# Branch prefetch hints for the experts' tile sizes, and the branch of the smallest tile put first where an expert ends

## The chip, the cores and the metric

The kernel runs on one core of a Trainium2 chip. The time is device microseconds of one execution, the median of several. Five engines take part, each with its own instruction stream: TensorE (PE in the profile, PEld for its weight loads and its sequencer), VectorE (DVE), ScalarE (ACT), GpSimd (POOL) and SyncE (SP).

## The reference

Causal block attention feeds a dense two-layer MLP, and its rows go through a top-1 mixture of eight experts. All is float32.

```python
def reference(...):
    x = attention(q, k, v)                       # 4 x 8 heads, 576 x 64 -> 2304 rows of 512
    h = x @ w_in; x = (max(h, 0) + alpha * min(h, 0)) @ w_out     # 512 -> 2048 -> 512
    logits = x @ w_gate                          # 8 experts
    expert = argmax(logits); gate = softmax(logits)[expert]
    for e in range(8):
        mask = expert == e
        if not mask.any():
            continue
        out[mask] = gate[mask] * (max(x[mask] @ w1[e], 0) @ w2[e])   # 512 -> 1024 -> 512
```

How many rows an expert gets depends on the data. With these inputs the experts get, from the largest to the smallest, 1366, 515, 296, 103 and 24 rows; three get none.

## The kernel before

Attention and the MLP are planned by a scheduler of the kernel's own (`Plan`) and are one straight run of instructions. The mixture behind it is written out by hand in `Experts.run`, with branches, and every branch is taken by all five engines, each for itself, on row counts that it has loaded into registers.

The experts are taken in order of their counts, r = 0 for the largest. An expert's rows are worked off in tiles: as many of 256 rows (`big`, `tile256`) as needed, and at its end one of 128 (`tile128`) or of 64 rows (`tile64`), which `small` picks. Three kinds of branches decide:

- `more` (L1157): has expert r more than 128 rows? If so a 256-row tile follows, otherwise `small`.
- `rest` (L1105): behind a 256-row tile, are there more than 128 rows left? If so another one, otherwise `small`.
- `few` (L1087): in `small`, are more than 64 rows left? If so the 128-row tile, otherwise the 64-row tile.

Besides, L1145 asks whether expert r has any rows, L1154 whether to load the weights of expert r + 2, L1093 (inside `small`) whether any row is left, and L1080 whether there is a next expert, whose rows are then fetched within the tile. Where a condition holds the code goes straight on; where it doesn't, the engine jumps over the whole arm. An arm that ends jumps over the other arm; that jump is in the profile as one more COMPARE_BRANCH of the arm's line.

The code is long because each (expert, tile, size) has its own copy. On TensorE a 256-row tile is some 310 instructions, one of 128 rows 115, one of 64 rows about 170; the 128- and 64-row copies for all places at which an expert may end stand behind the expert's chain of 256-row tiles.

With these counts the tiles are: five of 256 and one of 128 (r = 0), two of 256 and one of 64 (r = 1), one of 256 and one of 64 (r = 2), one of 128 (r = 3), one of 64 (r = 4). The first of them, tile (0, 0), is a straight piece ahead of the first branch.

Of the kernel before, what the change touches and what calls it, by code (L numbers as in the profile page):

```python
# [14 lines left out]
PSUM = bass.MemoryType.PSUM  # L15
DRAM = bass.MemoryType.DRAM
IOA = bass.IndirectOffsetOnAxis

P = 128
B, H, S, D = 4, 8, 576, 64  # L20
# [4 lines left out]
E, F2 = 8, 1024  # L25
# [646 lines left out]
class Route:  # L672
# [73 lines left out]
    def scatter(A, i):  # L746
        A.nc.gpsimd.indirect_dma_start(out=A.ml.info, out_offset=IOA(ap=A.si[:, i:i + 1], axis=0), in_=A.ig[:, i, :], in_offset=None)

# [74 lines left out]
class Experts:  # L823
# [58 lines left out]
    def fetch(A, r, j, base, rows=NT + 1):  # L882
        it = A.itile(r, j)
        A.nc.sync.dma_start(it, A.info[ds(base + 2 * P * j, 2 * P), :].rearrange("(h p) c -> p h c", p=P))
        for h in range(2):
            A.nc.gpsimd.indirect_dma_start(out=A.xg[:, h], out_offset=None, in_=A.x2[0:rows, :], in_offset=IOA(ap=it[:, h, 0:1], axis=0))

# [37 lines left out]
    def scatter(A, yo, it, h=0):  # L925
        n = yo.shape[0]
        A.nc.gpsimd.indirect_dma_start(out=A.out, out_offset=IOA(ap=it[0:n, h, 0:1], axis=0), in_=yo, in_offset=None, bounds_check=NT - 1, oob_is_err=False)  # L927

# [120 lines left out]
    def run(A, base, last, order, order_all):  # L1049

        nc = A.nc

        def reg(row, r, top):
            return nc.sync.value_load(order.ri[0:1, row, r:r + 1], min_val=0, max_val=top)

        def xpreps(r, j):
            return [lambda: A.xprep(r, j, 0), lambda: A.xprep(r, j, 1)]


        def nexts(r, j, b, nb):
            fs = xpreps(r, j) if b is not None else []
            if nb is not None:
                fs += [lambda: A.fetch(r + 1, 0, nb)] + [lambda: None] * (4 - len(fs)) + xpreps(r + 1, 0)
            return fs

        def big(r, j, b, jobs=(), nb=None):
            more = A.TOP[r] > 2 * P * (j + 1)
            if more:  # L1070
                A.fetch(r, j + 1, b)
            A.body(r, j, 2 * P, jobs, nexts(r, j + 1, b if more else None, nb))

        def small(r, j, n, jobs=(), nb=None, sure=False):

            def go(size):
                if nb is None:
                    A.body(r, j, size)
                    return
                with A.tc.If(ns[r + 1] > 0) as c:  # L1080
                    A.fetch(r + 1, 0, nb)
                    A.body(r, j, size, jobs, xpreps(r + 1, 0))
                with c.Else():
                    A.body(r, j, size)

            if A.TOP[r] - 2 * P * j > 64:
                with A.tc.If(n > 2 * P * j + 64) as c:  # L1087
                    go(P)
                with c.Else():
                    if sure:  # L1090
                        go(64)
                    else:
                        with A.tc.If(n > 2 * P * j):  # L1093
                            go(64)
            else:
                with A.tc.If(n > 2 * P * j):
                    go(64)

        def rest(r, j, n, b):
            if A.TOP[r] <= 2 * P * j:  # L1100
                return
            if A.TOP[r] <= 2 * P * j + P:
                small(r, j, n)
                return
            with A.tc.If(n > 2 * P * j + P) as c:  # L1105
                big(r, j, b)
                rest(r, j + 1, n, b)
            with c.Else():
                small(r, j, n)

        hold = {}

        def known():
            hold["e1"], hold["nb"] = reg(0, 1, E - 1), reg(2, 1, (E - 1) * NT)
            A.load_raws(1, hold["e1"])
            A.wtiles(1)

        def counts():
            _, hold["n"] = nc.values_load_multi_w_load_instructions(order.ri[0:1, 1, :], min_val=0, max_val=NT)

        A.body(0, 0, 2 * P, last + [lambda: A.fetch(0, 1, base), order_all, known, counts], [lambda: None] * 5 + xpreps(0, 1))
        nb = hold["nb"]
        e2, ns = reg(0, 2, E - 1), hold["n"]
        n0 = ns[0]

        def convs(r):
            return [lambda i=i: A.conv(r, i) for i in range(16)]

        def end():
            A.load_raws(2, e2)  # L1130

        with A.tc.If(n0 > 5 * P) as c:
            big(0, 1, base)
            big(0, 2, base, convs(1), nb)
            end()
            rest(0, 3, n0, base)
        with c.Else():
            with A.tc.If(n0 > 3 * P) as c:
                big(0, 1, base, convs(1), nb)
                end()  # L1140
                small(0, 2, n0)
            with c.Else():
                small(0, 1, n0, convs(1), nb, True)
                end()
        with ExitStack() as st:  # L1145
            for r in range(1, E):
                n, base = ns[r], nb
                st.enter_context(A.tc.If(n > 0))
                nb = reg(2, r + 1, (E - 1) * NT) if r < E - 1 else None
                jobs = convs(r + 1) if r < E - 1 else ()  # L1150

                def end():
                    if r < E - 2:
                        with A.tc.If(ns[r + 2] > 0):  # L1154
                            A.load_raws(r + 2, reg(0, r + 2, E - 1))

                with A.tc.If(n > P) as c:  # L1157
                    big(r, 0, base, jobs, nb)
                    end()
                    rest(r, 1, n, base)  # L1160
                with c.Else():
                    small(r, 0, n, jobs, nb, True)
                    end()


def moe_kernel(tc, q, k, v, w_in, w_out, alpha, w_gate, w1, w2, out):
    nc = tc.nc
    with ExitStack() as ctx:
# [112 lines left out]
        def fetch_rows():  # L1281
            ex = hold["ex"]
            it = ex.itile(0, 0)
            for h in range(2):
                nc.gpsimd.indirect_dma_start(out=ex.xg[:, h], out_offset=None, in_=x2[0:NT - G, :], in_offset=IOA(ap=it[:, h, 0:1], axis=0))

# [45 lines left out]
```

## Time and profile before

| | us |
|---|---|
| median of 3 runs | 1041.59 (1037.69 to 1044.52) |
| the profiled execution | 1040.76 |
| its span, first to last instruction | 1039.0 |
| TensorE busy | 934.6 (90%) |

The span is on one core, and the mean granted clock of TensorE is 0.938 of full. The rows of experts with branches begin some 755 us after the start of the span.

### The profile page before, as it was taken

To read this page: it belongs to the slowest core of one execution; us is meant where nothing else is said; L and a number is where in the kernel's file an instruction comes from. 1 tells how busy PE (TensorE), PEld (TensorE's weight loads), DVE (VectorE), ACT (ScalarE), POOL (GpSimd) and SP (SyncE) were. 2 spreads that over 40 slices of the span, in tenths; PEclk is the share of its full clock that TensorE was granted. 3 is DMA by queue.
4 is the path that set the end of the run, shared out by engine and by line. 5 is a ranking of instruction groups with operands and counts; after the bars stand their busy time and mean duration, and the time that the engine had idled before them with its cause. 6 is when DMAs were issued, how large, how long until landed. Compare 5 with 4: busy or idle time off the path is not lost. (4 is left out here: it accounts for less than half of the span.)

```text
span 1039.0 us, 18700 instructions
## 1 busy us (share of the span) xinstructions
PE 934.6 (90%) x6725; PEld 809.6 (78%) x6725; DVE 524.6 (50%) x1286; ACT 417.0 (40%) x1131; POOL 360.8 (35%) x429
## 2 busy tenths in 40 slices
PE   7884979999999999999999999998799999988554
PEld 6653868788788878888899999987688888877543
DVE  4898989554655645645443434455224314415130
ACT  5785554444544545545422121224124224325231
POOL 3556866332332333343322222232114212315030
PEclk8795998999899999999999999999999999999776
DMA  6553721112310121300010010033245212506110
GB/s 185 165 196 123 223 87 34 34 47 67 82 47 19 54 67 47 87 19 13 14 41 25 18 41 1 22 83 121 80 154 172 94 44 86 178 27 205 30 36 6
DMA packets 85296, 79.78 MB, mean 77 GB/s; under 512 B 53759, under 2 KB 65679, under 8 KB 85136
## 3 DMA queue, kind: packets, MB, share of 16 engines
q1 hardware_dynamic: 73984, 57.37, 19.0%
q0 software_dynamic: 4240, 11.56, 3.4%
q10 hardware_dynamic: 6912, 8.92, 2.4%
q8 instruction: 77, 1.26, 0.5%
q14 instruction: 83, 0.68, 0.2%
HBM read 63.49 MB, written 14.72 MB: 75 GB/s over the span
## 5 line engine op out<-in xcount | busy, mean ns | idle before, releaser
L578 PE MATMUL l<-xh,wi 128*128 128x256 f32 x1152 | 236.3, 290 | 1.9 <-DVE t L583 1.8
L578 PEld LDWEIGHTS l<-xh,wi 128*128 128x128 f32 x1152 | 191.6, 195 | 7.9 <-DVE t L583 2.7
L609 PE MATMUL acc<-wo,gh 128*128 128x512 f32 x576 | 191.7, 414 | 0.0
L578 PE MATMUL l<-xl,wi 128*128 128x256 f32 x576 | 165.3, 287 | 0.7 <-DVE xl L557 0.7
L589 POOL TENSOR_TENSOR gl<-t,gh 128x256 fp32r<-128x256 f32 x119 | 91.6, 770 | 193.9 <-ACT gh L586 163.0
L477 POOL TENSOR_SCALAR P<-P,sm 128x256 f32<-128x256 f32 (+4 forms) x89 | 102.2, 1152 | 162.4 <-DVE sm L450 70.2
L582 DVE TENSOR_SCALAR t<-l,al 128x256 f32<-128x256 f32 x144 | 69.5, 482 | 158.2 <-PE l L578 146.0
L586 ACT CAST gh<-t 128x256 fp32r<-128x256 f32 x144 | 58.5, 407 | 173.2 <-DVE t L583 75.5
L609 PE MATMUL acc<-wo,gl 128*128 128x512 f32 x288 | 113.9, 396 | 4.9 <-POOL gl L589 4.9
L578 PEld LDWEIGHTS l<-xl,wi 128*128 128x128 f32 x576 | 112.2, 195 | 4.6 <-DVE xl L557 1.3
L609 PEld LDWEIGHTS acc<-wo,gh 128*128 128x128 f32 x576 | 95.7, 190 | 16.1 <-issue 5.2
L465 PE MATMUL PT<-ident,P 128*128 128x128 f32 (+1 forms) x400 | 72.8, 297 | 27.3 <-DVE qlo L360 12.8
L470 ACT COPY F<-PT 128x256 f32<-128x256 f32 (+3 forms) x154 | 61.2, 415 | 74.3 <-PE PT L465 72.5
L465 PEld LDWEIGHTS PT<-ident,P 128*128 128x128 f32 (+1 forms) x400 | 48.7, 148 | 44.6 <-POOL P L477 10.9
L428 DVE TENSOR_REDUCE nb<-S 128x1 f32<-128x256 f32 (+4 forms) x160 | 70.9, 476 | 23.3 <-PE S L415 21.3
L499 PE MATMUL o<-F,v 128*64 128x128 f32 (+2 forms) x960 | 70.4, 279 | 2.3 <-ACT F L470 2.0
L609 PEld LDWEIGHTS acc<-wo,gl 128*128 128x128 f32 x288 | 54.3, 189 | 19.2 <-POOL gl L589 7.0
L442 ACT ACTIVATE P<-S,nb 128x128 f32<-128x128 f32 (+3 forms) x128 | 67.0, 532 | 5.6 <-DVE nb L428 3.0
L927 POOL DMA_INDIRECT out_dram<-yo,it x21 | 22.7, 1082 | 133.8 <-ACT yo L953 68.4
L499 PEld LDWEIGHTS o<-F,v 128*64 128x64 f32 (+1 forms) x960 | 50.0, 145 | 19.2 <-ACT F L470 5.5
L583 DVE SCALAR_TENSOR_TENSOR t<-l,t 128x256 f32<-128x256 f32 x144 | 61.1, 425 | 5.0
L880 DVE TENSOR_TENSOR e<-raw,e 128x512 fp32r<-128x512 f32 x44 | 39.8, 928 | 33.0 <-ACT e L879 33.0
(351 smaller groups left out, 1758.3 us busy)
## 6 DMA issues: line engine op xcount, KB each, us to landing
raw<-in_moe_w_dram SPq DMA_DIRECT2D x80, 256.0 KB
rawi<-in_moe_w_in_dram SPq DMA_DIRECT2D x16, 512.0 KB
rawo<-in_moe_w_out_dram SPq DMA_DIRECT2D x16, 512.0 KB
xr<-xT SPq DMA_DIRECT2D x9, 512.0 KB
v<-in_v_dram SPq DMA_DIRECT2D x32, 128.0 KB
x<-y ACTq DMA_DIRECT2D x16, 256.0 KB
xT<-xo ACTq DMA_DIRECT2D x16, 160.0 KB
q<-in_q_dram SPq DMA_DIRECT2D x20, 128.0 KB
```

What stands on the lines that cost most here:

```text
L428: nc.vector.tensor_reduce(pl["nb", p, c][:, j:j + 1], pl[Ss[j]][:, 0:N[j]], axis=AX.X, op=ALU.max, negate=True)
L442: nc.scalar.activation(pl[x][:, 0:N[j]], pl[Ss[j]][:, 0:N[j]], AF.Exp, bias=nb, scale=1.0, accum_out=pl["sm", p, c][:, j:j + 1])
L465: nc.tensor.transpose(pl[t][0:w, k], pl[x][:, P * k:P * k + w], A.K.ident)
L470: f(pl[F][:, 0:n], pl[t][:, 0:n])
L477: (nc.gpsimd if on == "POOL" else nc.vector).tensor_scalar(y, y, pl["sm", p, c][:, jj:jj + 1], None, op0=ALU.mult)
L499: nc.tensor.matmul(pl[o][r, 0:N], lhsT=v[0:w, 2 * kc + h], rhs=f, start=kc == 0, stop=kc == c, skip_group_check=True)
L578: nc.tensor.matmul(pl[l][:, 0:G], lhsT=a[:, c], rhs=b, start=k == 0 and j == 0, stop=k == 3 and j == 2)
L582: nc.vector.tensor_scalar(pl[t], x, 0.0, A.K.al[:, f:f + 1], op0=ALU.min, op1=ALU.mult)
L583: nc.vector.scalar_tensor_tensor(pl[t], x, 0.0, pl[t], op0=ALU.max, op1=ALU.add)
L586: nc.scalar.copy(pl[gh], pl[t])
L589: (nc.gpsimd if on == "POOL" else nc.vector).tensor_sub(pl[gl], pl[t], pl[gh].bitcast(F32))
L609: nc.tensor.matmul(pl[acc], lhsT=x[:, c], rhs=w, start=f == 0 and j == 0, stop=f == 15 and j == 2)
```

## The change

Each engine gets an instruction that announces a branch ahead of it (a branch prefetch hint), and for each one register operation that computes the condition from the row count. A hint is set for `few` and `more` of the next expert and for `few` and `rest` behind the tile, at the start of each 256-row tile, and for `few` and `more` of the next expert at the start of each 128- or 64-row tile. The conditions are those of the branches themselves, so that a hint says which way its branch will go. Besides, `few` asks the opposite question: the 64-row tile now follows its branch directly, and the 128-row tile stands behind it.

```diff
+        def hint(label, cond):
+            A.tc.mark_branch_hint_location(label, hint=cond, engines=ENGINES)
+
+        def hints(r, j):
+            if A.TOP[r] - 2 * P * j > 64 and (r, j) not in ((0, 0), (0, 1)):
+                hint(f"few{r}_{j}", hold["n"][r] <= 2 * P * j + 64)
+            if A.TOP[r] > 2 * P * j + P and j > (2 if r == 0 else 0):
+                hint(f"rest{r}_{j}", hold["n"][r] > 2 * P * j + P)
+            if j == 0:
+                hint(f"more{r}", hold["n"][r] > P)
...
         def big(r, j, b, jobs=(), nb=None):
             more = A.TOP[r] > 2 * P * (j + 1)
+            if r + 1 < E:
+                hints(r + 1, 0)
+            if more and (r, j) != (0, 1):
+                hints(r, j + 1)
...
             def go(size):
+                if r + 1 < E:
+                    hints(r + 1, 0)
...
             if A.TOP[r] - 2 * P * j > 64:
-                with A.tc.If(n > 2 * P * j + 64) as c:
-                    go(P)
-                with c.Else():
+                with A.tc.If(n <= 2 * P * j + 64, label=f"few{r}_{j}") as c:
                     if sure:
                         go(64)
                     else:
                         with A.tc.If(n > 2 * P * j):
                             go(64)
+                with c.Else():
+                    go(P)
...
-            with A.tc.If(n > 2 * P * j + P) as c:
+            with A.tc.If(n > 2 * P * j + P, label=f"rest{r}_{j}") as c:
...
-                with A.tc.If(n > P) as c:
+                with A.tc.If(n > P, label=f"more{r}") as c:
```

The change shifts line numbers by up to 20: in the changed kernel `few` is L1107, L1093 is L1111, L1080 is L1100, `more` is L1177, and the register operations of the hints are L1064.

First place: TensorE, the start of expert r = 2 (`more` and tile (2, 0)). In a tile's name the first number is j, the second the size.

```order
L1154 UNCONDITIONAL_BRANCH x2
L1145 COMPARE_AND_BRANCH
L1157 COMPARE_AND_BRANCH
L923 MATMUL l_0_256+_0_16350<-cxh_7054,e_0_8919 128x256
L923 MATMUL l_0_256+_0_16350<-cxl_7055,e_0_8919 128x256
```

The same place in the changed kernel:

```order
L1174 UNCONDITIONAL_BRANCH x2
L1165 COMPARE_AND_BRANCH
L1177 COMPARE_AND_BRANCH
L1064 REGISTER_ALU
L1347 BRANCH_PREFETCH_HINT
L1064 REGISTER_ALU
L1347 BRANCH_PREFETCH_HINT
L1064 REGISTER_ALU
L1347 BRANCH_PREFETCH_HINT
L924 MATMUL l_0_256+_0_18250<-cxh_7054,e_0_8919 128x256
```

Three pairs stand where `big` calls for four hints: those of `few` for a tile j above 0 have no instruction in the built program; the last pair of the three is `rest`'s.

Second place: TensorE, the end of the 128-row copy of tile (2, 1) and the start of its 64-row copy, before:

```order
L923 MATMUL Y_1_128_17530<-e_15_9193,hh_7060 128x512 x2
L923 MATMUL Y_1_128_17530<-e_15_9193,hl_7061 128x512
L1087 UNCONDITIONAL_BRANCH
L1093 COMPARE_AND_BRANCH
L1006 MATMUL H_1_64_0_17568<-e_0_8919,cxh_7056 128x256 x2
L1006 MATMUL H_1_64_0_17568<-e_1_8951,cxh_7056 128x256 x2
```

And the start of `small` for tile (2, 1) in the changed kernel:

```order
L1107 COMPARE_AND_BRANCH
L1111 COMPARE_AND_BRANCH
L1064 REGISTER_ALU
L1347 BRANCH_PREFETCH_HINT
L1064 REGISTER_ALU
L1347 BRANCH_PREFETCH_HINT
L1007 MATMUL H_1_64_0_19697<-e_0_8919,cxh_7056 128x256 x2
```

The 64-row tile has moved from behind the 128-row tile to right behind the branch.

Third place: TensorE, `small` for tile (3, 0), the 128-row tile of the fourth expert, before:

```order
L1087 COMPARE_AND_BRANCH
L1080 COMPARE_AND_BRANCH
L923 MATMUL H_0_128+_0_19122<-e_0_9445,cxh_7054 128x512 x2
L923 MATMUL H_0_128+_0_19122<-e_0_9445,cxl_7055 128x512
L923 MATMUL H_0_128+_0_19122<-e_1_9446,cxh_7054 128x512 x2
```

And after the change:

```order
L1107 COMPARE_AND_BRANCH
L1064 REGISTER_ALU
L1347 BRANCH_PREFETCH_HINT
L1064 REGISTER_ALU
L1347 BRANCH_PREFETCH_HINT
L1100 COMPARE_AND_BRANCH
L1007 MATMUL H_0_64+_0_21717<-e_0_9445,cxh_7054 128x256 x2
```

What followed the branch here was the 128-row tile that these counts run; now it is the 64-row tile, and the 128-row tile is reached by a jump over both 64-row copies.

## Rows read from the trace of the kernel before

**Rows 1.** The page, part 1: busy time and share of TensorE.

```profile
PE 934.6 (90%) x6725; PEld 809.6 (78%) x6725; DVE 524.6 (50%) x1286; ACT 417.0 (40%) x1131; POOL 360.8 (35%) x429
```

**Rows 2.** Waits, 845 to 1039 us: waiter, releaser, us in total, times, longest.

```profile
PE H L1006 <- issue: 21.7, 3, 11.6
...
PE H_128+_0_19122 L923 <- issue: 8.0, 2, 7.1
...
PE l_256+_0_16350 L923 <- ACT e L879: 1.7, 1, 1.7
...
PE l_256+_0_13102 L923 <- ACT yo L993: 1.0, 1, 1.0
```

**Rows 3.** Timeline of TensorE, four stretches: start, us, tile, [idle before <-releaser].

```profile
919.67 1.54 PE L1006 MATMUL H<-e,cxh 128*128 128x256 f32 x11 [2.73 <-issue]
...
965.23 0.98 PE L1006 MATMUL H<-e,cxh 128*128 128x256 f32 x3 [7.39 <-issue]
...
983.63 1.19 PE L923 MATMUL H_128+_0_19122<-e,cxh 128*128 128x512 f32 x2 [7.09 <-issue]
...
986.17 1.01 PE L923 MATMUL H_128+_0_19122<-e,cxh 128*128 128x512 f32 x2 [0.92 <-issue]
...
1011.63 1.62 PE L1006 MATMUL H<-e,cxh 128*128 128x256 f32 x6 [11.59 <-issue]
```

**Rows 4.** Single branches of TensorE's sequencer, by line: min/median/max ns, start.

```profile
L1105 PEldq COMPARE_BRANCH  x1: 3509/3509/3509, 912.6 to 912.6; - x1
L1087 PEldq COMPARE_BRANCH  x1: 3206/3206/3206, 916.2 to 916.2; - x1
L1105 PEldq COMPARE_BRANCH  x1: 4238/4238/4238, 956.2 to 956.2; - x1
L1087 PEldq COMPARE_BRANCH  x1: 4410/4410/4410, 960.5 to 960.5; - x1
L1093 PEldq COMPARE_BRANCH  x1: 3693/3693/3693, 974.4 to 974.4; - x1
L1157 PEldq COMPARE_BRANCH  x1: 4742/4742/4742, 978.3 to 978.3; - x1
L1087 PEldq COMPARE_BRANCH  x1: 65/65/65, 983.1 to 983.1; - x1
L1080 PEldq COMPARE_BRANCH  x1: 3568/3568/3568, 996.4 to 996.4; - x1
L1157 PEldq COMPARE_BRANCH  x1: 4388/4388/4388, 1000.5 to 1000.5; - x1
L1087 PEldq COMPARE_BRANCH  x1: 3328/3328/3328, 1004.9 to 1004.9; - x1
L1080 PEldq COMPARE_BRANCH  x1: 2962/2962/2962, 1008.3 to 1008.3; - x1
L1154 PEldq COMPARE_BRANCH  x6: 65/189/255, 891.4 to 1021.4; - x6
```

**Rows 5.** Instruction transfers on queue q8, 600 to 700 us and 975 to 1012 us: packets, MB, share.

```profile
q8 instruction: 5, 0.08, 0.3%
...
q8 instruction: 10, 0.16, 2.3%
```

**Rows 6.** Register operations of SyncE at one line: min/median/max ns.

```profile
L869 SPq FUSED_REGOPS  x16: 37/46/51, 937.5 to 959.3; - x16
```

**Rows 7.** Timeline of ScalarE, 977 to 1014 us.

```profile
1000.14 0.69 ACT L993 ACTIVATE yo<-Y_128+_19175,it 128x512 f32<-128x512 f32 x1
1013.80 0.37 ACT L1032 COPY s<-H 128x256 f32<-128x256 f32 x1 [12.97 <-PE H L1006]
```

**Rows 8.** Windows: stretch, us, busy of PE, PEld, DVE, ACT, POOL, then granted clock, DMA.

```profile
854.00:868.00 14.00, 13.22 (x61) 10.31 (x59) 1.38 (x2) 3.75 (x6) 1.01 (x1) 1.00 0.06 23
...
965.00:977.00 12.00, 11.32 (x80) 11.14 (x80) 1.64 (x5) 3.17 (x10) 0.00 (x0) 0.83 0.01 3
1011.00:1024.00 13.00, 11.91 (x80) 11.73 (x80) 1.64 (x5) 3.17 (x10) 0.00 (x0) 0.78 0.01 4
```

More of the change, by code (lines that the diff above doesn't have):

```diff
@@ L17 @@
 IOA = bass.IndirectOffsetOnAxis
+ENGINES = [getattr(mybir.EngineType, e) for e in ("PE", "DVE", "Activation", "Pool", "SP")]
 P = 128
```

## The prediction

> **What bounds the kernel now.** I read the page first: TensorE is busy for 90% of the span [rows 1], so only its idle time can be won, and the change touches only the last 120 us, where the experts of few rows lie. So the second view is the list of waits there [rows 2]. Two groups stand out, 21.7 us in three waits ahead of a 64-row tile's first product and 8.0 us in two waits ahead of the 128-row tile. Both carry the releaser "issue": no other engine and no transfer holds TensorE up, it has no instruction yet. The third view, TensorE's timeline, gives them places [rows 3]: I call them C (tile (1, 2), 2.73 us), E (tile (2, 1), 7.39), F (tile (3, 0), 7.09 and 0.92) and G (tile (4, 0), 11.59). Two smaller waits, B and D, stand at the start of a 256-row tile and end with ScalarE [rows 2].
>
> The fourth view says what the engine does meanwhile: single branches [rows 4]. One that doesn't jump takes 65 ns, a short jump up to 255 ns, and each jump over a tile's copy takes 2.96 to 4.74 us. Instruction transfers go with them: 5 packets of 16 KB in 100 us of straight code, 10 in 37 us of the branches around F and G [rows 5]. A far jump thus costs a fetch.
>
> The sequencer stands ahead of the matrix unit, and that hides a part. At C the first of two long branches starts at 912.6 while the unit has work until 919.67 − 2.73 = 916.94, a lead of 4.3 us; in the same way the lead is 1.6 us at E, 2.1 at F and 3.6 at G [rows 3, 4]. The long branches less this lead give the idle time: at E 4.24 + 4.41 − 1.6 = 7.0 of 7.39; at F 3.69 + 4.74 − 2.1 = 6.3, and with the step to the next code 7.09; at G 3.57 + 4.39 + 3.33 + 2.96 − 3.6 = 10.7 of 11.59.
>
> The Trainium skill ("Advanced Engine Details and Errata", Control Flow Timing) gives a compare-and-branch about 108 ns. The 65 ns rows agree with it in size, the 3 to 4.7 us rows don't; by it nothing here could be won and the time would stay at 1041.
>
> **The change, part by part.** Two edits act in different ways.
>
> *The order of the arms.* At C, E and G `few` finds at most 64 rows; it jumped, for 3.21, 4.41 and 3.33 us, and now falls through for 0.065 as it did at F [rows 4]. At F it is the other way round: 65 ns become a jump over two 64-row copies, 3.2 us by the nearest row (the jump at C), bounds 2.96 and 4.74. The 128-row tile (3, 0) is now last in its part, so that the jump at its end, L1080 at 996.4, crosses one copy of 115 instructions; I take it for short, 0.2 us in place of 3.57, and hold it possible that it stays. The second L1080, 2.96 at 1008.3, has in the changed code no arm of another size between it and its target, only the tile's other copy of 170 instructions; I take 0.2 here too, bounds 0.2 and 2.96.
>
> *The hints.* A hint can only save the fetch of a branch that jumps. These are `rest` at C and E (3.51, 4.24), `more` at F and G (4.74, 4.39) and the new jump of `few` at F. No row shows a hint at work. The bounds for a hinted jump are 0.2 us (code on hand, the short jump) and the full row. `rest`'s hint is the last one set in its tile, and a whole 256-row tile lies between it and its branch: I take 0.2. `more`'s hint is set one tile ahead and has another jump, L1111 or L1100, between itself and its branch; I assume that the code a hint has brought does not wholly survive that, and take the middle: 3.0 at F, 2.0 at G. `few` at F is announced ahead of `more` in the same tile; I assume that the later hint takes its place, and give it the full 3.2. These two assumptions are the choice that the sum rests on.
>
> *What the hints cost.* Three pairs at the start of a 256-row tile, two at the start of a small one. The nearest rows are a register operation, 46 ns [rows 6], and the branch of 65 ns [rows 4]. But from that branch's start at 983.1 to the first product at 983.63 are 0.5 us, so an instruction may cost more than its record. I take 0.12 each, 0.7 for three pairs and 0.5 for two, bounds zero (inside the lead) and 1.5. Within a tile a lead of 1.6 us or more hides it; where TensorE already waits for its instructions it does not: at F, B and D. Hints on the other four engines stand behind the same branches and have more slack there. No hint waits for anything, and no DMA issue changes its place.
>
> Now the places, each against its idle time:
> - C: the two branches fall from 6.7 us to 0.3, the lead of 4.3 covers them: −2.7.
> - E: from 8.65 to 0.3 and 0.5 of hints, the lead of 1.6 covers that, bar some 0.4: −7.0. The weights of tile (2, 1) are there since tile (2, 0), so nothing else is late.
> - F: −1.7 for `more`, +3.1 for `few`, +0.3 for the hints, −0.9 for the second wait, whose code is no longer the next in line: +0.8.
> - G: the chain falls from 14.2 to 2.5, below the lead. Next to be late is ScalarE: its last activation of tile (3, 0) ends at 1000.83, and then it has branches of its own before it can read the first H [rows 7]. If `more` takes it 2 to 2.5 us, TensorE loses 1 to 1.5 waiting for room: −10.1.
> - B and D: +0.7 each.
>
> Sum −17.6 us of idle time.
>
> *The clock.* Behind these idle stretches TensorE's granted clock is lower: a 64-row tile with its 80 products is busy for 11.32 us at 0.83 behind E and 11.91 at 0.78 behind G, while a tile without an idle stretch ahead of it ran at 1.00 [rows 8]. Busy time times clock is 9.4 and 9.3, so at 1.00 the two would give back 2.0 and 2.6, and 4.6 is the upper bound, zero the lower. F stays, and G's tile runs soon after it; I take 2.5.
>
> The profiled execution took 1040.76, 0.8 below the median. 1040.8 − 17.6 − 2.5 = 1020.7: I forecast **1021**. With the bounds of `more` and the clock it runs from 1016 to 1026.
>
> **The rivals.**
>
> *1. The hints bring nothing, and only the order acts.* No row speaks against it. `rest` and `more` keep their rows: C −2.6, E −4.35 with 0.45 of hints −3.9, F −0.9 + 3.2 + 0.5 = +2.8, G −9.1 (4.39 for `more` less the lead, and ScalarE behind its own), B and D +1.4: −11.4, clock −1.5: 1028.
>
> *2. Every hint is kept until its branch.* Then `more` and `few` at F take 0.2 each: −4.5 for `more` and +0.2 for `few`, with the second wait −5.0 in place of +0.8; −23.4, clock −4: 1013.
>
> *3. Slower: a hinted fetch displaces what the engine runs next.* Each tile starts by announcing a jump of the next expert, mostly one that is far off. If the code that it brings takes the place of the tile's own continuation, this has to be fetched back in the middle of the tile, where the rows price a fetch at 3 to 4.7 us. With 12 branched tiles at 3 us that is 36 us against 20 won. It decides from 7 tiles exposed on; at half of them the time is 1039, at all 1057. Speaking for it: instruction transfers come about once per 20 us of straight code [rows 5], one or none in a tile, so little is held at a time. Against: TensorE's lead hides a part.
>
> The Trainium skill ("Runtime: NRT & Kernel Launch", Instruction fetch mechanics) states that the instruction store is refilled in blocks of 16 KiB, straight ahead, and that a jump out of its window waits for the fetch. The 16 KB packets and the long jumps agree; what a hint does there it doesn't say, and with a store so small rival 3 would be the outcome, at 1057 or nearer to it.
>
> *4. Given back.* The wins at E and G pass to ScalarE, GpSimd or a transfer that is just behind, or the far jumps lie elsewhere in the new layout: 1036 ± 5. Speaking for it: at G ScalarE was idle for 12.97 us, but only because TensorE was late [rows 7]. Against: weights and rows of the next expert come a whole tile ahead.
>
> **How the numbers follow.** Chances: forecast 0.52, rival 1 0.18, rival 2 0.09, rival 3 0.12, rival 4 0.09. The range that leaves out no more than 2 in 10 takes in the forecast, rivals 1 and 2 and the lower edge of rival 4: 1010 to 1034. The measurement can tell a change of about 1%, so 1030.4 is the bound of faster: the forecast, rival 2 and nearly all of rival 1, 0.77. Between the bounds: rival 4, the rest of rival 1 and a quarter of rival 3, 0.14. Slower: the rest of rival 3, 0.09.
>
> **What would show it.** Right: TensorE's branch records of `rest` (L1125) near 0.2 us at tiles (1, 2) and (2, 1); `few` (L1107) 65 ns at C, E and G and some 3 us at F; `more` (L1177) 2 to 3 us at F and G; the waits at C and E gone, at G below 1.5 us, F near 8.8; a granted clock above 0.9 in tile (2, 1). `rest` at 3.5 and 4.2 us means rival 1; `more` and `few` at F both short means rival 2; new waits on issue in the middle of 256-row tiles, and clearly more packets on q8, mean rival 3. The forecast is wrong above all if the far jumps I hold for short, L1100 at F's end, are not.

## The result and the profile after

| | before | changed |
|---|---|---|
| median | 1042.46 us (6 runs, 1037.69 to 1047.99) | 1024.81 us (6 runs, from 1024.06) |
| ratio | | 0.9836, 95% interval 0.9807 to 0.9865 |
| the profiled execution | 1040.76 us | 1024.06 us |
| its span | 1039.0 us | 1022.3 us |
| TensorE's mean granted clock | 0.938 | 0.953 |

The changed kernel is 1.6% faster. One of its six runs took 1749.35 us, far above all the others: the median in the table counts it, the ratio does not, and the median of the other five is 1024.45 us, 18.0 below the kernel before. The page shows the same work as before: TensorE has 6725 products and is busy 930.8 us, against 934.6 [rows 1].

```profile
PE 930.8 (91%) x6725; PEld 806.9 (79%) x6725; DVE 524.5 (51%) x1286; ACT 417.0 (41%) x1131; POOL 360.6 (35%) x429
```

TensorE's waits among the experts, 840 to 1025 us, answer to [rows 2] (waiter, releaser, us, times, longest):

```profile
PE H_128+_0_21997 L924 <- DVE e L881: 9.3, 1, 9.3
PE H L1007 <- DVE e L881: 3.1, 1, 3.1
PE l_256+_0_18250 L924 <- ACT e L880: 2.5, 1, 2.5
PE l_256+_0_14072 L924 <- issue: 1.9, 1, 1.9
PE Th L1016 <- ACT s L1033: 1.6, 1, 1.6
```

The group of 21.7 us ahead of the 64-row tiles has shrunk to one wait of 3.1, at G. C and E have gone. F is 9.3 where it was 8.0. Two things are new: G now ends with VectorE, and inside tile (1, 2) TensorE waits 1.6 us for ScalarE. The timeline of TensorE puts them in place and answers to [rows 3]:

```profile
914.88 2.06 PE L1007 MATMUL H<-e,cxh 128*128 128x256 f32 x16
918.57 0.66 PE L1016 MATMUL Th<-II,s 128*128 128x64 f32 x4 [1.63 <-ACT s L1033]
...
957.30 2.05 PE L1007 MATMUL H<-e,cxh 128*128 128x256 f32 x16
...
976.41 1.19 PE L924 MATMUL H_128+_0_21997<-e,cxh 128*128 128x512 f32 x2 [9.26 <-DVE e L881]
...
994.90 3.66 PE L1007 MATMUL H<-e,cxh 128*128 128x256 f32 x16 [3.15 <-DVE e L881]
```

The first product of tile (1, 2), at 914.88, and that of tile (2, 1), at 957.30, have no bracket: TensorE did not stop. The branches of its sequencer say why; they answer to [rows 4], place by place (C, E, F, G):

```profile
L1125 PEldq COMPARE_BRANCH  x1: 362/362/362, 910.7 to 910.7; - x1
L1107 PEldq COMPARE_BRANCH  x1: 67/67/67, 911.1 to 911.1; - x1
L1125 PEldq COMPARE_BRANCH  x1: 348/348/348, 955.9 to 955.9; - x1
L1107 PEldq COMPARE_BRANCH  x1: 72/72/72, 956.3 to 956.3; - x1
L1111 PEldq COMPARE_BRANCH  x1: 3672/3672/3672, 965.0 to 965.0; - x1
L1177 PEldq COMPARE_BRANCH  x1: 2904/2904/2904, 968.9 to 968.9; - x1
L1107 PEldq COMPARE_BRANCH  x1: 3744/3744/3744, 971.9 to 971.9; - x1
...
L1177 PEldq COMPARE_BRANCH  x1: 442/442/442, 988.8 to 988.8; - x1
L1107 PEldq COMPARE_BRANCH  x1: 77/77/77, 989.4 to 989.4; - x1
L1100 PEldq COMPARE_BRANCH  x1: 233/233/233, 989.9 to 989.9; - x1
```

`rest` (L1125) went from 3.51 and 4.24 us to 0.36 and 0.35, `few` (L1107) at C, E and G to 0.07, `more` (L1177) at G from 4.39 to 0.44 and the second L1100 to 0.23 (the first, at 988.1, to 0.21). F is the row of three long jumps that is left: 3.67, 2.90 and 3.74 us in a row, from 965.0 to 975.6, with TensorE out of work since 967.15. So F is a wait for code, although the list names VectorE: its conversion happened to end at 975.5, the later of the semaphores that the first product also waits for.

At G it is really VectorE. Its timeline shows the conversions of the last expert's weights end at 994.76, and TensorE begins at 994.90; its own sequencer had been through its branches since 990.1.

```profile
974.82 0.68 DVE L881 TENSOR_TENSOR e<-raw,e 128x512 fp32r<-128x512 f32 x1
982.87 0.69 DVE L881 TENSOR_TENSOR e<-raw,e 128x512 fp32r<-128x512 f32 x1 [7.37 <-ACT e L880]
...
989.49 5.27 DVE L881 TENSOR_TENSOR e<-raw,e 128x512 fp32r<-128x512 f32 x5
```

The conversions are jobs inside tile (3, 0). VectorE stands for 7.37 us between two of them, from 975.50 to 982.87, behind F and not during it: it waits for ScalarE's half of the next conversion, which in ScalarE's order comes behind that tile's first activation, at 981.73. Windows of the tiles, with the clock (the last three numbers are granted clock, DMA share, GB/s), answer to [rows 8]:

```profile
930.40:954.60 24.20, 24.09 (x150) 21.74 (x150) 11.63 (x18) 11.53 (x21) 10.72 (x9) 0.94 0.54 167
...
956.00:967.50 11.50, 11.15 (x87) 10.47 (x85) 3.70 (x7) 5.27 (x14) 2.42 (x2) 1.00 0.37 127
...
994.50:1006.50 12.00, 11.19 (x80) 11.01 (x80) 1.90 (x6) 3.12 (x10) 0.00 (x0) 0.86 0.08 25
```

Tile (2, 1) (second row) now runs at full clock and takes 9.85 us (957.30 to 967.15) instead of 11.32; tile (4, 0) has 0.86 and 11.19 instead of 0.78 and 11.91. Tile (2, 0) (first row) lost some of it, 24.09 us at 0.94, while in the trace of before this tile was busy for 22.71 us at 1.00 (the row below). The loss does not follow from the longer wait at D: few_last and pe_only, two kernels of the next section, wait 2.4 and 2.2 us there and run this tile at 1.00 in 22.7 us.

```profile
932.40:955.20 22.80, 22.71 (x150) 20.40 (x150) 13.13 (x18) 11.54 (x21) 11.33 (x10) 1.00 0.59 180
```

One caution on spans: the 16.7 us between the two profiled executions are not all the change's. The third `rest` stands at 850.78 us before and at 848.19 after, and the stretch ahead of it has a wait of 1.81 us for fetched rows in the one trace and none in the other. Over all profiled executions of this study the third `rest` lay between 845 and 857 us, whatever was changed. From it to TensorE's last product are 172.8 us before (850.78 to 1023.54) and 157.9 after (848.19 to 1006.09): −14.9. Traces are compared by this stretch, the **tail** below; whether a kernel is faster is read from the ratios.

### The profile page after: what moved, and what is told of

The parts are those of the page before. It is cut to its first block, busy times and chain, and to the rows that moved or that the text cites. A ratio compares the mean times of both kernels' runs of the same rounds, so it can differ in the third digit from the quotient of the medians.

```text
span 1022.3 us, 18992 instructions
## 1 busy us (share of the span) xinstructions
PE 930.8 (91%) x6725; PEld 806.9 (79%) x6725; DVE 524.5 (51%) x1286; ACT 417.0 (41%) x1131; POOL 360.6 (35%) x429
```

## The experiments

All kernels below come from the changed kernel. Ratios are to the kernel before, run beside them. In the first group the question is which of the two edits does it.

**order_only**: every hint left out, the arms as changed.

```diff
-            A.tc.mark_branch_hint_location(label, hint=cond, engines=ENGINES)
+            pass
```

> The changed order of few's arms without any hint. Theory: the two edits act apart, and the hints of rest bring their code in. Then without them TensorE's branch of rest takes 3 to 4.5 us again at tiles (1, 2) and (2, 1); the lead hides it at C, at E some 3 to 4 us of idle time come back, and few's branch falls through (65 ns) at C, E and G as in the changed kernel. At F more takes up to 4.7 us in place of 2.9, few some 3.5, the hints' 0.5 us go: F 9 to 11 us. At G more takes some 4 us, which VectorE's conversion (the end of the wait there) covers. Time 1028 to 1031. Rival (the order does all, the hints nothing): rest stays near 0.35 us as a matter of the layout, time 1024 to 1026 as the changed kernel.

Ratio 0.9961 [0.9929, 0.9993]: 4 us, much less than I expected. Tail 171.1 us. Branches of TensorE (`rest` and `few` at A, `rest` at E, `more` and `few` at F, L1100 at G) and its waits:

```profile
L1125 PEldq COMPARE_BRANCH  x1: 3524/3524/3524, 853.9 to 853.9; - x1
L1107 PEldq COMPARE_BRANCH  x1: 3609/3609/3609, 857.5 to 857.5; - x1
L1125 PEldq COMPARE_BRANCH  x1: 4245/4245/4245, 965.1 to 965.1; - x1
L1177 PEldq COMPARE_BRANCH  x1: 5706/5706/5706, 982.5 to 982.5; - x1
L1107 PEldq COMPARE_BRANCH  x1: 4722/4722/4722, 988.3 to 988.3; - x1
L1100 PEldq COMPARE_BRANCH  x1: 3161/3161/3161, 1010.2 to 1010.2; - x1
```

```profile
PE H_128+_0_19377 L924 <- issue: 12.4, 1, 12.4
PE H L1007 <- issue: 8.5, 2, 5.3
PE H L924 <- issue: 3.0, 1, 3.0
```

E is 3.1 us, as expected (8.5 is E and G together, G 5.3). The third row is a place that the prediction left out: **A**, the end of the first expert, whose last tile has 128 rows. There `few` fell through before; turned round it jumps for 3.61 us, and behind `rest`'s 3.52 that is more than the lead. F is 12.4 us, since `more` and `few` together take 10.4. So the order alone wins some 4 us at E, 6 at G and 1 at C, and gives 3 back at A, 4 at F and half a microsecond each at B and D.

**hints_only**: the hints, with few's arms in the old order and the condition to match.

```diff
-                with A.tc.If(n <= 2 * P * j + 64, label=f"few{r}_{j}") as c:
+                with A.tc.If(n > 2 * P * j + 64, label=f"few{r}_{j}") as c:
+                    go(P)
+                with c.Else():
                     ...
-                with c.Else():
-                    go(P)
```

> All hints, with few's arms in the old order (128-row tile first). Theory: rest stays short (0.4 us), few jumps at C, E and G again for 3.2 to 4.4 us: C is covered by the lead, E idles some 3 us, F gains because few falls through (9.3 us to 5.5), and at G the jump of L1100, more and few stand in a row: 6 to 8 us in place of 3.15. Time about 1029. Rival (the order does all): 1040 to 1042, as before the change. Rival (every hint is kept until its branch): few of expert 4 is short at G, G as in the changed kernel, time 1023 to 1025.

Ratio 0.9897 [0.984, 0.9954], tail 164.1 us. `rest` is short, and `few` jumps again, here at E and at G:

```profile
L1125 PEldq COMPARE_BRANCH  x1: 346/346/346, 954.0 to 954.0; - x1
L1107 PEldq COMPARE_BRANCH  x1: 4274/4274/4274, 954.4 to 954.4; - x1
L1107 PEldq COMPARE_BRANCH  x1: 3579/3579/3579, 994.2 to 994.2; - x1
```

E 3.8, F 5.3, G 7.4 us, and 1.7 more inside tile (4, 0): the places as expected. The rival that the order does it all is out, and so is the one that every hint is kept, for `few` of expert 4 is hinted one tile ahead and still takes 3.58 us. Order alone 4 us, hints alone 11, together 17: within the intervals the two edits add up.

**rest_only**: the changed order, and of the hints those of `rest` alone.

```diff
-                hint(f"few{r}_{j}", hold["n"][r] <= 2 * P * j + 64)
+                pass
...
-                hint(f"more{r}", hold["n"][r] > P)
+                pass
```

> The changed order and the hints of rest alone; those of few and more are left out. Theory: rest short at both places, E without idle time; at G more takes some 4 us, covered by VectorE's conversion; at F more takes 3 to 4.7 us without a hint and the hints' instructions go (0.5 us): F 8.8 to 10.5 us. Time 1024 to 1026, within 0.2% of the changed kernel. Rival (the hints of few and more carry a good part): more 4.4 us or longer at both places and the time 1028 or above.

Ratio 0.9832 [0.9768, 0.9896], tail 156.7 us: no difference from the changed kernel. `more` goes back to its old length at F and G,

```profile
L1177 PEldq COMPARE_BRANCH  x1: 4579/4579/4579, 975.1 to 975.1; - x1
L1177 PEldq COMPARE_BRANCH  x1: 3666/3666/3666, 996.2 to 996.2; - x1
```

and it costs nothing: at F 9.7 us, with `few` at 3.0 there, and at G the same 3.1 us for VectorE, which hides `more` whole. The hints of `few` and `more` are worth nothing here that can be told.

Beside order_only this run shows something more. The hints of `rest` take 3.0 us from A and 3.1 from E. But F is 2.8 us and G 2.2 us shorter too, though no hint is set for a branch there: at F `more` takes 4.58 us instead of 5.71 and `few` 3.04 instead of 4.72, at G the jump L1100 takes 0.23 instead of 3.16. So some 5 us of what the hints seem to bring are jumps that no hint announces and that are shorter in this kernel's layout; why they are shorter is not shown.

In the second group the question is why some hints act and others don't.

**few_last**: the hint of `few` moved behind that of `more`.

```diff
-            if A.TOP[r] - 2 * P * j > 64 and (r, j) not in ((0, 0), (0, 1)):
-                hint(f"few{r}_{j}", hold["n"][r] <= 2 * P * j + 64)
             ...
             if j == 0:
                 hint(f"more{r}", hold["n"][r] > P)
+            if A.TOP[r] - 2 * P * j > 64 and (r, j) not in ((0, 0), (0, 1)):
+                hint(f"few{r}_{j}", hold["n"][r] <= 2 * P * j + 64)
```

> As the changed kernel, with the hint of few behind that of more at each tile's start, so that few's is the later of the two at a small tile. If of several hints only the last one set acts, more at G (0.44 us in the changed kernel) goes back to 3 to 4.4 us, covered by VectorE there. At F two outcomes: if a hint's code is on hand once fetched, few at F falls from 3.75 to 0.2 us, F from 9.3 to 6 us and the time to 1021; if the far jumps between the hint and its branch undo it (my theory), few stays at 3 to 4 us and the time at 1024 to 1026. If all hints act whatever their order, more stays at 0.44 us at G.

Ratio 0.9819 [0.9765, 0.9873], tail 157.6 us. `more` and `few` at F, and `more` at G:

```profile
L1177 PEldq COMPARE_BRANCH  x1: 4622/4622/4622, 975.1 to 975.1; - x1
L1107 PEldq COMPARE_BRANCH  x1: 3630/3630/3630, 979.8 to 979.8; - x1
L1177 PEldq COMPARE_BRANCH  x1: 3581/3581/3581, 996.4 to 996.4; - x1
```

`more` at G, 0.44 us when its hint is the last, is 3.58 when `few`'s is. And at F `few` has gained nothing by being last (3.63 against 3.74), with two far jumps between hint and branch.

**rest_first**: at the start of a 256-row tile the hint of `rest` ahead of the next expert's two. No instruction of another kind moves, so that the code's layout is the changed kernel's.

```diff
+            if more and (r, j) != (0, 1):
+                hints(r, j + 1)
             if r + 1 < E:
                 hints(r + 1, 0)
-            if more and (r, j) != (0, 1):
-                hints(r, j + 1)
```

> The changed kernel with rest's hint ahead of the next expert's two at the start of each 256-row tile, nothing else; every instruction keeps its place. Theory (of several hints only the last one set acts): rest's branch takes 3.3 to 4.3 us again at the ends of the chains, as without hints. At A rest and few jump one behind the other, 6.5 to 7 us, some 3 us of idle time; at C the lead covers rest; at E 3 to 4 us idle; F and G as in the changed kernel. The work from the first branch to the last product, 252.7 us in the changed kernel, becomes some 259, and the ratio 0.987 to 0.992. Rival (all hints act, whatever their order): rest stays at 0.35 to 0.41 us and the ratio at 0.980 to 0.986.

Ratio 0.9883 [0.9853, 0.9914]. `rest` at A, C and E, and `more` at F and G:

```profile
L1125 PEldq COMPARE_BRANCH  x1: 3627/3627/3627, 846.5 to 846.5; - x1
L1125 PEldq COMPARE_BRANCH  x1: 3542/3542/3542, 915.4 to 915.4; - x1
L1125 PEldq COMPARE_BRANCH  x1: 3790/3790/3790, 959.8 to 959.8; - x1
...
L1177 PEldq COMPARE_BRANCH  x1: 3453/3453/3453, 977.1 to 977.1; - x1
L1177 PEldq COMPARE_BRANCH  x1: 442/442/442, 997.3 to 997.3; - x1
```

A idles 3.6 us, E 3.0; from the first branch (751.2) to the last product (1014.5) are 263.2 us, where I expected 259, and the changed kernel has 252.7 (753.4 to 1006.1). With nothing else moved this is the cleanest of the runs: the same hint, set two hints earlier, is lost. (The trace has 7.4 us more idle time in the tail than the changed kernel's, and 2.7 us more busy time at a lower clock, 0.92 against 0.94.)

**pe_only**: the hints on TensorE alone.

```diff
-ENGINES = [getattr(mybir.EngineType, e) for e in ("PE", "DVE", "Activation", "Pool", "SP")]
+ENGINES = [mybir.EngineType.PE]
```

> The changed kernel with the hints on TensorE alone. Theory: it is TensorE's own wait for code that the hints take away, and on the other engines rest's branch is as long with its hint as without (at C ScalarE 2.5 us to the next instruction after the change, 2.8 before): ratio 0.980 to 0.988, the changed kernel's. Waits as in the changed kernel: E none, F 9 to 10 us, G some 3 us. Rival (the other engines' hints carry a part, above all more at G on ScalarE and VectorE, 0.4 us with the hint): G longer by 2 to 3 us, since VectorE converts the last weights behind that branch, and the time 1027 to 1029.

Ratio 0.9800 [0.9776, 0.9824], tail 155.9 us; F 8.6, G 3.1 us, E none. Nothing is lost without the other four engines' hints, not even at G, where VectorE ends the wait.

The third group tries what is left at F and G.

**few3_old**: few's old order for expert 3 alone.

```diff
+                if r == 3:
+                    with A.tc.If(n > 2 * P * j + 64, label=f"few{r}_{j}") as c:
+                        go(P)
                     ...
```

> The changed kernel with the arms of few in the old order for expert 3 alone, where the 128-row tile follows. Theory: the order edit costs at F what its jump takes (3.0 to 3.8 us) since no hint reaches it: F falls from 9.3 to 5.5 us. At G the jump at the 128-row tile's end (L1100, 475 instructions) takes 3.5 us again, and more behind it loses its hint to that jump in part (2.5 to 3.5 us): the chain is some 7 us less the lead of 3.6, so G grows from 3.15 to 4 us. Sum -2.5 to -3 us: ratio 0.980. Rival (F is bound by something else than few's jump): F stays at 9 us and the ratio at 0.983 to 0.988.

Ratio 0.9829 [0.9799, 0.986], tail 154.3 us (849.05 to 1003.31). F 6.2 and G 4.1 us: the −3 at F and +1 at G that were expected, in the trace; in the median no difference that can be told.

**more_inv_few_last**: `more` turned round for experts 3 and up, and few's hint last.

```diff
+                if r < 3:
                     ...
+                else:
+                    with A.tc.If(n <= P, label=f"more{r}") as c:
+                        small(r, 0, n, jobs, nb, True)
+                        end()
+                    with c.Else():
+                        big(r, 0, base, jobs, nb)
+                        end()
+                        rest(r, 1, n, base)
```

> The changed kernel with more's arms turned round for experts 3 and up (the small tile follows the branch), its condition turned too, and the hint of few set last in a small tile. At F only the arm-end jump L1111 now lies between few's hint and its branch. Theory: more falls through at F, -2.9 us. few's jump of 361 instructions now stands where more's stood in the changed kernel, behind one far jump with the last hint, and so takes some 3 us or less in place of 3.75: F 5.5 to 6.5 us. If a hint survives a far jump wholly, few takes 0.2 us and F is 3 us. At G a far jump over the expert's 256-row copies is new (3.5 us), more and few fall through: covered by VectorE. Ratio 0.979 to 0.982 (0.977 if the hint survives).

Ratio 0.9826 [0.98, 0.9852], tail 153.0 us. F is 6.0 us, with `few` at 3.17: with a far jump between hint and branch the hint brings little or nothing (without a hint `few` took 3.04 us there in rest_only and 4.72 in order_only). G is 4.1 us and ends with issue, not covered by VectorE as I had expected.

**rest_inv_few3**: the last two together, with the hints of `rest` alone.

```diff
-                hint(f"few{r}_{j}", hold["n"][r] <= 2 * P * j + 64)
+                pass
...
-                hint(f"more{r}", hold["n"][r] > P)
+                pass
```

> The hints of rest alone, few's 64-row tile first but for expert 3, and more turned round for experts 3 and up: at F no far jump is left but L1121 at the end of tile (2, 1). Theory: F falls from 9.3 to some 2.5 us (a jump of 3.6 us less the lead of 2.1, and short branches). At G two far jumps in a row (475 and 1510 instructions) take 7 us less the lead of 3.6, so 3.5 to 4.5 us, against 3.15. Time 1018 to 1020, ratio 0.975 to 0.978. Rival (behind the branches the weights' conversion or the fetched rows are late for tile (3, 0)): F stays above 6 us, ended by VectorE, ScalarE or a transfer, and the ratio near 0.983.

Ratio 0.9790 [0.9767, 0.9812], tail 157.1 us; the profiled execution, 1028.11 us, is the slowest of its five. F falls to 1.9 us as expected. G does not stay at 4:

```profile
L1184 PEldq COMPARE_BRANCH  x2: 231/2754/5277, 987.5 to 987.8; - x2
L1100 PEldq COMPARE_BRANCH  x1: 3439/3439/3439, 984.0 to 984.0; - x1
L1100 PEldq COMPARE_BRANCH  x1: 2768/2768/2768, 993.5 to 993.5; - x1
```

```profile
986.44 0.40 PE L924 MATMUL Y_128+_18453<-e,hl 128*128 128x512 f32 x1
996.63 0.77 PE L1007 MATMUL H<-e,cxh 128*128 128x256 f32 x2 [9.79 <-issue]
```

Three far jumps stand there now, in order of time L1100 with 3.44 us, L1184 with 5.28 and L1100 with 2.77. The jumps saved at F have come back at G.

**pe_inv**: more_inv_few_last with the hints on TensorE alone.

```diff
-ENGINES = [getattr(mybir.EngineType, e) for e in ("PE", "DVE", "Activation", "Pool", "SP")]
+ENGINES = [mybir.EngineType.PE]
```

> The kernel with more turned round for experts 3 and up and few's hint last, with the hints on TensorE alone: a try for a faster version than the changed kernel. Theory: F some 6 us and G 3 to 4 us as in that kernel, and the hints of the other engines are worth nothing: some 249 us from the first branch to the last product (252.7 in the changed kernel), ratio 0.977 to 0.982. Rival (the other engines' hints are worth something with this order): waits on VectorE or ScalarE grow and the ratio is above 0.983.

Ratio 0.9785 [0.9755, 0.9815], median 1018.78 us; 245.6 us from the first branch (751.8) to the last product (997.4), F 5.4, G 3.8 us.

It is the best median of the study and faster than the kernel before beyond doubt; against the changed kernel its interval overlaps (0.9807 to 0.9865), so that the step from the one to the other is likely, not shown.

## Why the prediction held, point by point

The forecast was 1021, the measurement 1024.8. In the traces, the tail lost 14.9 us where the working had −20.1; 13.8 of it are TensorE's idle time (33.2 us before, 19.5 after) and 1.1 its busy time (139.5 and 138.4).

- **C, −2.7 forecast.** The 2.73 us went, and 1.63 came back inside the tile, as a wait for ScalarE. Its `rest` branch is as long with its hint as without (2.5 us to its next instruction, 2.8 before), and pe_only shows nothing lost without it (1.4 us there). I had priced the other engines' branches only at G; that was a miss of 1.6 us.
- **E, −7.0.** Right: −7.4, with `rest` at 0.35 and `few` at 0.07.
- **F, +0.8.** Measured +1.25. `more` 2.90 where 3.0 was taken, `few` 3.74 where 3.2 was.
- **G, −10.1.** Measured −8.4. The chain of branches fell further than forecast (`more` 0.44, not 2.0), but the step "next to be late is ScalarE, 1 to 1.5 us" failed: it is VectorE, with the weights' conversions, 3.15 us. rest_only shows how firm that is: with `more` at 3.67 G is the same 3.1. The trace of before already had it: TensorE's last product of tile (3, 0) ended at 1000.04 (1011.63 − 11.59 [rows 3]) and VectorE's last conversion at 1003.03, hidden then by the branches.

```profile
997.77 5.26 DVE L880 TENSOR_TENSOR e<-raw,e 128x512 fp32r<-128x512 f32 x5
```

This distance of 3.0 us is the same in eleven of the twelve traces (3.4 in rest_inv_few3), and in none is G below 3.1.
- **B and D, +0.7 each.** Measured +0.9 each. The three pairs take 0.56 us of it at either place. Their records are short, but each instruction begins some 0.09 us behind the one before (at B from 865.99 to 866.55), where 0.12 was taken. The rest is the long jump ahead of them, which the working left as it was: at B 3.65 us after 3.26, at D 3.66 after 3.34. order_only, without a hint, has 1.6 and 2.2 us there, with jumps of 3.85 and 3.87. The records:

```profile
L1064 PEldq ALU_OP  x28: 33/37/42, 753.5 to 989.7; - x28
```

```profile
L1347 PEldq BRANCH_PREFETCH_HINT  x30: 28/35/49, 753.6 to 989.8; - x30
```

- **The clock, −2.5.** Measured −1.1 of busy time: tiles (2, 1) and (4, 0) gave 1.5 and 0.7 back, but tile (2, 0) lost 1.4, which the working didn't have.
- **The two assumptions** on which the sum rested, that the last of several hints takes the place of the earlier ones, and that a far jump between hint and branch undoes it, were choices without a row. rest_first and few_last show the first one: `rest` 0.35 or 3.8 us, `more` at G 0.44 or 3.58, by nothing but the order of the hints. The second is shown in part: `few` behind far jumps is never below 2.9 us. `more` at F, last and behind one far jump, took 2.90, 3.00, 3.04, 3.45 and 3.44 us in five kernels, 4.58, 4.62 and 5.71 in three where it was not hinted or not last. In three of these kernels the code lies in the same place (2.90 and 3.45 with the hint last, 4.62 with it first): so something survives, 1 to 2 us.
- **Rival 1** ("the hints bring nothing", 1028) is refuted, and its price was wrong too: the order by itself is worth 4 us, not 13. Its working left A out, took `more` and `few` at F for no longer than they were, while both were at their worst there (5.71 and 4.72), and had no far jump at L1100 of G, which took 3.16.
- **Rival 2** falls with hints_only, few_last and rest_first. **Rival 3** (displaced code) shows nowhere: there is no new wait in a 256-row tile, and the instruction transfers of the experts' stretch (750 to 1010 us) are fewer, 28, where before there were 35 from 750 to 1026.

```profile
q8 instruction: 28, 0.46, 0.8%
```

Rival 4 (given back) is true in small: C's 1.63 us and G's 3.15 are such waits, behind the ones that went.

The unhinted far jumps take 2.4 to 5.7 us in every trace here. The Trainium skill ("Runtime: NRT & Kernel Launch", Instruction fetch mechanics) says that a jump out of the fetched window waits for the target page; these rows agree.

The forecast also drew 1021 from a profiled execution of 1040.76, and the changed one was 1024.06, with 2.6 us of its gain ahead of the third `rest`, outside the change. So part of the nearness is luck: the steps of the working, taken together, promised 5.2 us more than the tail lost.

## What to carry to other kernels

On TensorE a far jump is worth a hint where it stands alone: set the hint last, within the straight stretch that ends at the branch, and expect nothing of a hint that another one follows, and little of one with another far jump between. The order of the arms moves a jump rather than removing it, and a new layout changes the length of jumps that no edit was meant for, so look at every place that shares the code, the ones now hidden too (A), before counting a gain. When a wait of 10 us goes, ask for every engine what it does in that time: here VectorE's conversions kept a quarter of it at G, and ScalarE's own branch over half of it at C.

## What had not been expected of the hardware

- The same jump within tile (4, 0), over 187 instructions, took 0.23 us in the changed kernel and 3.16 in order_only, 2.37 in pe_inv, 2.72 in more_inv_few_last and 2.77 in rest_inv_few3. So its length does not set its time. Its place in the program differs, and a boundary between fetched pieces (16 KB each on q8) would explain that; no run was made to settle it.
- Only TensorE's hints are worth anything here in the time (pe_only, 0.9800). On ScalarE `rest` at C took 2.5 us to the next instruction with its hint and 2.5 without it (pe_only), while the same hint on TensorE took its branch from 3.51 to 0.36 us. On VectorE it was 3.0 in the changed kernel, 2.8 in pe_only and 0.5 in rest_only, where no other hint is set. At A ScalarE's `rest` took 0.45 us to the next instruction in the kernel before and in pe_only and 2.7 in the changed kernel. Why is open, and so is whether the hints or the place of the code do it.
